# Second half's layernorm for the MLP made on x as features by tokens, with the tokens' moments sent through DRAM

## The chip, the cores and the metric

The kernel runs on one core of one Trainium2 chip. The metric is the device time of one execution in microseconds (us); the time shown for a kernel is the median of its runs. The core has five engines: TensorE (PE, with its weight loads shown apart as PEld), VectorE (DVE), ScalarE (ACT), GpSimd (POOL) and SyncE (SP). SP and POOL issue the DMA transfers here, each in the order of its own program.

## What is computed

The input x has 2048 tokens of 512 features, in fp32. Everything is made of its layernorm xn:

```python
xn = (x - mean(x)) / sqrt(var(x) + 1e-5)          # per token, over 512 features
a, b = xn @ Wd_re.T, xn @ Wd_im.T                 # DFT over the features
s = Ws_re @ a - Ws_im @ b                         # real part of the DFT over the tokens
g = silu((sigmoid(xn @ w_gate) * (xn @ w_up)) @ w_down)      # 512 -> 1792 -> 512
out = x + s * g
```

The MLP's matmuls contract over features, so xn is needed there with features on the partitions (features by tokens). The DFT over the tokens contracts over tokens, so there xn is needed with tokens on the partitions. The input array `x` is tokens by features; `x_t` holds the same x as features by tokens (8 pieces of 128 x 2 x 512) and before this change is read only for the residual at the end.

## The kernel before

**Arithmetic.** Every fp32 operand is split into a high part (`split`, L66, on ACT) and the rest (L67, on DVE), and a product is three matmuls of the parts (`mm3`, L70 to L72: high by high, high by rest, rest by high). Blocks of two by two are multiplied with seven products in place of eight; the sums and differences that this takes are DVE work (`combine`, L118; `x_sum`, L215).

**Stages.** Tokens come in two halves `h` of 1024, hidden features in seven groups `g` of 256. For half 0, group 0 is written out by hand (`start`), and its x is normalised and transposed there. Groups 1 to 6 of half 0 are six blocks (`block_units`) of nine units each, 54 units in all. Then come seven groups of half 1, the DFT over the tokens (`seq_units`) and the DFT over the features with the end (`hidden_units`).

**Order.** The program is a list of units written out by hand; a unit is 12 or 24 matmuls (a gate-up product `u1`, `u3`, `u5`, `u7`, `u8`, or a piece of the last group's down product, `carried`). `after(n, f)` puts the work `f` behind unit n, `sooner(n, f)` ahead of it. Ahead of each unit the loads of the next five units are issued and the operands of the next two are split. Engines run their own part of that program in order, and wait for each other through semaphores. All tiles in SBUF are 53 pages of 128 x 1024 fp32; a load waits until the page that it was given is free, so SP's queue runs ahead of the other engines as far as pages come free.

**The second half's x.** While half 0's blocks run, the eight tiles of 128 tokens of half 1 (`i` from 8 to 15) are prepared, two per block, around units m = 6, 15, 24 and 33 (the last lines of the kernel, L978 to L987):

- `fetch` (L147): loads x, tokens by features;
- `norm_a` (L155 to L158, behind unit m - 4): mean and variance on DVE into the tile `mv`, then on POOL the sum with eps (L157) and the power -0.5 (L158) into `rs`;
- `norm_b` (L163, behind unit m - 2): DVE makes (x - mean) * scale in place;
- `turn` (L176, behind unit m): four transposes on TensorE per tile, into a PSUM bank of the tag "pd". The down products use the same two "pd" banks;
- `keep_raw` (L187, behind unit m): ACT copies the bank into two pages `xraw[1, j, b]` (j is the pair of feature blocks, b the 512 tokens);
- `store_xn` (L169, behind unit m + 1): POOL stores the normalised tile to DRAM (`xn_part`) for the DFT over the tokens.

From unit 49 on, `xraw` is split and summed into half 1's operands (L66, L67, L215).

Of the kernel before, what the change touches and what calls it, by code (L numbers as in the profile page):

```python
# [8 lines left out]
F32 = mybir.dt.float32  # L9
F32R = mybir.dt.float32r  # L10
AF = mybir.ActivationFunctionType
ALU = mybir.AluOpType
ADD, SUB = ALU.add, ALU.subtract

P = 128
# [5 lines left out]
KH = NS // NH  # L21
NT = S // 512
SB = 512
# [8 lines left out]
def fnet_glu_kernel(ctx: ExitStack, tc: tile.TileContext, x, x_t, c_re, c_im, w_h, w_gu, w_down, out):  # L32
    nc = tc.nc
    PSUM = bass.MemoryType.PSUM

    const = ctx.enter_context(tc.tile_pool(name="const", bufs=1))
    stat = ctx.enter_context(tc.tile_pool(name="stat", bufs=4))
    pages = ctx.enter_context(tc.tile_pool(name="pages", bufs=PAGES))
    dram = ctx.enter_context(tc.tile_pool(name="dram", bufs=1, space=bass.MemoryType.DRAM))
    banks = ctx.enter_context(tc.tile_pool(name="banks", bufs=1, space=PSUM))  # L40

    def page(shape, dtype=F32R):
        return pages.tile([P, *shape], dtype, name="page")

    def bank(tag):
        return banks.tile([P, 512], F32, name=tag, bufs=2 if tag == "pd" else 1)
# [5 lines left out]
    mhalf = const.tile([P, 1], F32, name="mhalf")  # L52
    nc.gpsimd.memset(mhalf, -0.5)
    warm = const.tile([P, 1], F32, name="warm")
    nc.scalar.activation(warm, mhalf, AF.Sigmoid)
    xn_part = dram.tile([2, 2, 2, P, 4, D // 2], F32, name="xn_part")
    g_part = [dram.tile([P, 2, SB], F32, name=f"g_part{i}") for i in range(2 * NT)]
    ws_part = dram.tile([NG, 2, P, 2, 4 * P], F32, name="ws_part")
# [64 lines left out]
    xraw = {}  # L123
# [8 lines left out]
    def after(n, f):  # L132
        extra.setdefault(n, []).append(f)

    def sooner(n, f):
        early.setdefault(n, []).append(f)


    xs = {}

    def fetch(i, hold=False):
        pg = page([2, D], F32)
        if hold:
            nc.vector.memset(pg[:, 0, :1], 0.0)
        for j in range(2):
            xs[i + j] = pg[:, j, :]
            nc.sync.dma_start(xs[i + j], x[(i + j) * P : (i + j + 1) * P, :])  # L147

    st_of = {}

    def norm_a(i):
        st = stat.tile([P, 6], F32, name="st")
        mv = stat.tile([P, 2], F32, name="mv")
        rs = stat.tile([P, 2], F32, name="rs")
        nc.vector.bn_stats(st, xs[i])  # L155
        nc.vector.bn_aggr(mv, st)
        nc.gpsimd.tensor_scalar(rs[:, 0:1], mv[:, 1:2], EPS, None, op0=ALU.add)  # L157
        nc.gpsimd.tensor_tensor(rs[:, 1:2], rs[:, 0:1], mhalf, op=ALU.pow)  # L158
        st_of[i] = mv, rs

    def norm_b(i):
        mv, rs = st_of.pop(i)
        nc.vector.tensor_scalar(xs[i], xs[i], mv[:, 0:1], rs[:, 1:2], op0=ALU.subtract, op1=ALU.mult)  # L163

    def store_xn(i):

        q, p = divmod(i // 2, 4)
        to = xn_part[q, i % 2, :, :, p, :].rearrange("d p c -> p d c")
        nc.gpsimd.dma_start(to, xs.pop(i).rearrange("p (d c) -> p d c", d=2))  # L169
# [3 lines left out]
    def turn(i):  # L173
        turned[i] = bank("pd").rearrange("p (d s) -> p d s", d=ND)
        for d in range(ND):
            nc.tensor.transpose(turned[i][:, d, :], xs[i][:, d * P : (d + 1) * P], ident)  # L176

    def place(i):
        h, b, o = i // 8, i % 8 // 4, i % 4
        return [(h, j, b) for j in range(2)], slice(o * P, (o + 1) * P)  # L180

    def keep_raw(i):
        keys, at = place(i)
        for j, k in enumerate(keys):
            if k not in xraw:
                xraw[k] = page([2, SB], F32)
            nc.scalar.activation(xraw[k][:, :, at], turned[i][:, 2 * j : 2 * j + 2, :], AF.Copy)  # L187
# [17 lines left out]
    def x_sum(h, k):  # L205

        if (h, k) not in xsum:
            xsum[h, k] = page([2, SB], F32)
        a, b = {
            1: lambda: (xraw[h, 0, 1], xraw[h, 0, 0]),  # L210
            2: lambda: (xraw[h, 1, 1], xsum[h, 1]),
            3: lambda: (xraw[h, 1, 1], xraw[h, 0, 1]),
            4: lambda: (xraw[h, 1, 0], xsum[h, 2]),
        }[k]()
        nc.vector.tensor_tensor(xsum[h, k], a, b, op=SUB)  # L215
# [172 lines left out]
    class Seven:  # L388
# [56 lines left out]
        def run(self, k):  # L445
            first = k in (2, 1, 5)
            if first:
                self.ps = [bank("pd") for _ in range(2)]
            hv, wv = self.h[k].get(), self.weights(k)
            for o, ps in enumerate(self.ps):  # L450
                mm3(ps, [t[:, o * P : (o + 1) * P] for t in wv], hv, first, True, go_on=not first)
            (b, i), sign = {
                2: ((0, 0), 1),
                1: ((0, 0), 1),
                6: ((1, 0), -1),
                7: ((1, 1), -1),
                4: ((0, 1), 1),
                5: ((1, 1), 1),
                3: ((1, 0), 1),
            }[k]  # L460
            gather(0 if self.g == 0 and k in (2, 6, 7, 4) else 1, [((2 + b) * 2 + i, ps) for ps in self.ps], sign)
# [64 lines left out]
    def start(h, g):  # L526
# [43 lines left out]
        def begin():  # L570
# [7 lines left out]
            fetch(0)  # L578
            loads[0].load()
            norm_a(0)  # L580
            fetch(2, hold=True)
            loads[1].load()
            fetch(4)
            fetch(6)
            for p in units[0][0] + units[2][0]:
                p.load()
            wdl.load()
            norm_a(1)
            w_hi(0, 0)
            norm_b(0)  # L590
            turn(0)
            busy(2, 256)
            keep_hi(0)
            norm_b(1)
            turn(1)
            busy(4, 256)
            keep_hi(1)
            w_hi(0, 1)
            w_lo(0, 0)
            norm_a(2)  # L600
            w_lo(0, 1)
            norm_a(3)
# [49 lines left out]
    def c_blocks(tc_, pp):  # L652
        b = {(j, m): Load(c[tc_, j, pp], [2, SB]) for j in range(2) for m, c in enumerate((c_re, c_im))}
        return [b[k] for k in ((0, 0), (0, 1), (1, 0), (1, 1))]

    def xn_blocks(q):
        a = {(d, j): Load(xn_part[q, j, d], [4, D // 2]) for d in range(2) for j in range(2)}
        return [a[k] for k in ((0, 0), (0, 1), (1, 0), (1, 1))]
# [18 lines left out]
    def sums_ahead(n, make, blocks, to, at=(3, 5, 6, 8)):  # L677

        steps = make(*blocks, to)

        def step(dst, a, b, op, to):
            v = combine(dst(), a.get(), b.get(), op)
            nc.gpsimd.dma_start(to, v)

        for i, v in enumerate(blocks):
            sooner(n + i // 2, v.load)
        for i, v in enumerate(steps):
            after(n + at[i], lambda v=v: step(*v))
# [271 lines left out]
    with tc.manual_schedule():  # L960
        job, begin = start(0, 0)
        for i in range(KH):
            after(i // 2, lambda i=i: store_xn(i))
        for h in range(NH):
            n = len(units)
            for g in range(NG):
                m = len(units)
                if h and g:
                    job = late_units(h, g, job)
                elif h:  # L970
                    job = block_units(h, g, job, [], Seven(g))
                elif g:
                    job = block_units(h, g, job, [])
                if h == 0 and g in (1, 2):
                    sums_ahead(m, sums, c_blocks(0, g - 1), t_part[g - 1])
                elif h == 0 and g in (4, 5):
                    sums_ahead(m, diffs, xn_blocks(g - 4), s_part[g - 4])
            if h == 0:  # L978
                n = len(units)
                for i in range(KH):  # L980
                    m = 9 * (i // 2) + 6
                    if i % 2 == 0:
                        after(m - 6, lambda i=i: fetch(KH + i))
                    after(m - 4, lambda i=i: norm_a(KH + i))
                    after(m - 2, lambda i=i: norm_b(KH + i))
                    after(m, lambda i=i: (turn(KH + i), keep_raw(KH + i)))
                    after(m + 1, lambda i=i: store_xn(KH + i))  # L987
                for i, k in {-5: 1, -4: 2, 0: 6, 1: 5}.items():
                    sooner(n + i, xop[1, k].get)
                for i, k in {-3: 1, -2: 2, 1: 3, 2: 4}.items():  # L990
                    after(n + i, lambda k=k: x_sum(1, k))
            else:
                seq_units(job)
        hidden_units()
        begin()
        for n, (needs, run) in enumerate(units):
            now[0] = n
            for f in early.get(n, []):
                f()
            for k in range(n, min(n + LOAD_AHEAD + 1, len(units))):  # L1000
                for p in units[k][0]:
                    p.load()
            for k in range(n, min(n + SPLIT_AHEAD + 1, len(units))):
                for p in units[k][0]:
                    p.get()
            run()
            for f in extra.get(n, []):
                f()
# [52 lines left out]
```

## Time and profile before

| what | value |
|---|---|
| median of 3 runs | 821.48 us (821.05 to 822.24) |
| the profiled execution's own time | 822.36 us |
| its span, from the first to the last recorded instruction | 820.6 us |
| TensorE busy | 809.8 us, 99% of the span |
| VectorE / ScalarE / GpSimd busy | 645.2 / 490.9 / 144.0 us |
| DMA | 207.27 MB, mean 253 GB/s |
| granted TensorE clock | 0.999 |

"Busy" counts the instructions' own durations. Matmuls are pipelined: each is recorded for about 0.39 us but the next starts 0.227 us later, so the starts tell what a matmul costs, not the durations. Times in the views count from the start of the span; a "releaser" is what ended an engine's idle time; "landing" is the time from a DMA's issue to its arrival.

### The profile page before, as it was taken

Reading aid. Unit: us, or ns where it says so; the run is one execution under the profiler, and the core shown is the slowest. Engines: PE = TensorE matmul, PEld = TensorE weight load, DVE = VectorE, ACT = ScalarE, POOL = GpSimd, SP = SyncE. Lnnn points to the kernel's source line nnn. Section 1 sums busy time; section 2 is a strip of 40 time slices with the busy share of each in tenths; the row PEclk is TensorE's granted clock in tenths of the full one; section 3 lists DMA queues with packets and bytes.
Section 4 is the critical chain, followed back from the end, with each engine's and each line's share of the span. In section 5 each row is a group of like instructions: output and inputs, shape, how many; then the busy total and the mean of one; then the engine's idle time right before and its main releaser. Section 6 shows DMA issues by size and latency. Waiting matters only on the chain.

```text
span 820.6 us, 10472 instructions
## 1 busy us (share of the span) xinstructions
PE 809.8 (99%) x3686; PEld 673.2 (82%) x3686; DVE 645.2 (79%) x814; ACT 490.9 (60%) x762; POOL 144.0 (18%) x214
## 2 busy tenths in 40 slices
PE   8999999999999999999999999999999999999997
PEld 7988888888878888888888888888888888888786
DVE  6798867757788867876797796889888976988946
ACT  4666655655677888887787773544355545535441
POOL 2143422322111122212121100011101110002201
PEclk9999999999999999999999999999999999999999
DMA  8349999699677888998999997358937994799984
GB/s 317 144 170 401 272 257 285 186 321 309 163 175 165 228 179 214 251 200 199 280 291 311 265 347 271 134 209 309 310 146 287 341 394 150 253 316 395 304 275 77
DMA packets 59253, 207.27 MB, mean 253 GB/s; under 512 B 6592, under 2 KB 6848, under 8 KB 59200
## 3 DMA queue, kind: packets, MB, share of 16 engines
q0 software_dynamic: 25072, 87.57, 42.1%
q1 hardware_dynamic: 34128, 119.03, 40.2%
q8 instruction: 29, 0.48, 0.2%
q14 instruction: 24, 0.20, 0.1%
HBM read 122.16 MB, written 88.08 MB: 256 GB/s over the span
## 4 chain that ended last, share of the span: by engine, by line
PE 93%; DVE 3%; ACT 1%; DMA 1%; issue 1%; POOL 0%; SPq 0%; DVEq 0%
PE pd L70 6%; PE pd L71 6%; PE pd L72 6%; PE ga L70 5%; PE ga L72 5%; PE ua L72 5%; PE ua L71 5%; PE ga L71 5%; PE ua L70 5%; PE gc L70 3%; PE gc L72 3%; PE gc L71 3%; PE uc L72 3%; PE uc L70 3%; PE uc L71 3%; PE gb L72 3%
## 5 line engine op out<-in xcount | busy, mean ns | idle before, releaser
L67 DVE TENSOR_TENSOR page<-page 128x1024 fp32r<-128x1024 f32 (+1 forms) x340 | 322.0, 978 | 116.0 <-ACT page L66 114.5
L66 ACT ACTIVATE page<-page 128x1024 fp32r<-128x1024 f32 (+1 forms) x340 | 276.1, 859 | 91.8 <-DVE page L118 72.1
L118 DVE TENSOR_TENSOR page<-page 128x1024 f32<-128x1024 f32 (+2 forms) x184 | 169.2, 935 | 8.0 <-DMA page<-xn_part 5.9
L291 ACT ACTIVATE page<-pd 128x512 f32<-128x512 f32 x154 | 89.5, 595 | 62.7 <-PE pd L72 59.4
L295 POOL DMA_DIRECT2D g_part<-page x69 | 60.1, 889 | 277.2 <-ACT page L291 220.6
L70 PE MATMUL pd<-page 128*128 128x512 f32 x242 | 94.3, 390 | 0.8 <-DVE page L898 0.8
L71 PE MATMUL pd<-page 128*128 128x512 f32 x242 | 94.2, 389 | 0.0
L72 PE MATMUL pd<-page 128*128 128x512 f32 x242 | 94.2, 389 | 0.0
L70 PE MATMUL ga<-page 128*128 128x512 f32 x200 | 78.1, 391 | 0.8 <-ACT page L308 0.8
L72 PE MATMUL ga<-page 128*128 128x512 f32 x200 | 77.9, 390 | 0.0
L72 PE MATMUL ua<-page 128*128 128x512 f32 x200 | 77.9, 390 | 0.0
L71 PE MATMUL ga<-page 128*128 128x512 f32 x200 | 77.9, 389 | 0.0
L70 PE MATMUL ua<-page 128*128 128x512 f32 x200 | 77.9, 389 | 0.0
L71 PE MATMUL ua<-page 128*128 128x512 f32 x200 | 77.9, 389 | 0.0
L70 PEld LDWEIGHTS pd<-page 128*128 128x128 f32 x242 | 45.4, 188 | 10.7 <-issue 1.2
L72 PEld LDWEIGHTS pd<-page 128*128 128x128 f32 x242 | 45.4, 188 | 9.4
L71 PEld LDWEIGHTS pd<-page 128*128 128x128 f32 x242 | 45.4, 188 | 9.4
L70 PE MATMUL ub<-page 128*128 128x512 f32 (+1 forms) x126 | 48.3, 383 | 0.5 <-DVE page L940 0.5
L70 PE MATMUL gc<-page 128*128 128x512 f32 x124 | 48.6, 392 | 0.0
L71 PE MATMUL gc<-page 128*128 128x512 f32 x124 | 48.3, 390 | 0.0
L72 PE MATMUL gc<-page 128*128 128x512 f32 x124 | 48.3, 389 | 0.0
L70 PE MATMUL uc<-page 128*128 128x512 f32 x124 | 48.3, 389 | 0.0
(135 smaller groups left out, 1351.9 us busy)
## 6 DMA issues: line engine op xcount, KB each, us to landing
g_part<-page POOLq DMA_DIRECT2D x77, 512.0 KB, 7.8
page<-in_c_re_dram SPq DMA_DIRECT2D x36, 512.0 KB, 6.3
page<-f_part SPq DMA_DIRECT2D x36, 512.0 KB, 5.5
page<-in_c_im_dram SPq DMA_DIRECT2D x34, 512.0 KB, 6.0
page<-in_w_gu_dram SPq DMA_DIRECT2D x28, 512.0 KB, 7.6
f_part<-page POOLq DMA_DIRECT2D x28, 512.0 KB, 6.9
page<-in_w_down_dram SPq DMA_DIRECT2D x14, 512.0 KB, 8.7
page<-xn_part SPq DMA_DIRECT2D x14, 512.0 KB, 8.4
```

The source lines that it names most:

```text
L66: nc.scalar.activation(hi, src, AF.Copy)
L67: nc.vector.tensor_tensor(lo, src, hi.bitcast(F32), op=SUB)
L70: nc.tensor.matmul(ps, ws[0], ms[0], start=first, stop=False, skip_group_check=go_on)
L71: nc.tensor.matmul(ps, ws[0], ms[1], start=False, stop=False, skip_group_check=go_on)
L72: nc.tensor.matmul(ps, ws[1], ms[0], start=False, stop=last, skip_group_check=go_on)
L118: (engine or nc.vector).tensor_tensor(dst, a, b, op=op)
L291: nc.scalar.activation(pg[:, o, :], po, AF.Copy, scale=float(sign))
L295: nc.gpsimd.dma_start(g_part[i], pg, accum_op=ADD)
```

## The change

For half 1, `xraw` is no longer made by transposing the normalised tiles. It is loaded from `x_t` and normalised in place, features by tokens.

- `norm_a` for half 1 copies the mean on POOL (a new instruction) and writes the scale beside it, into a small tile `moments` of 128 x 2 x 8. `norm_b` and `store_xn` stay, with the mean and scale from `moments`.
- `turned_half(12, 0)` and `turned_half(30, 1)` prepare 512 tokens each. Behind unit 12 (30) POOL stores the means and the scales of four tiles to DRAM, `m_part[b]`: two DMAs of 128 x 4 single fp32 elements, each element to an address of its own, so that tokens lie in a row.
- Ten units later, ahead of unit 22 (40), SP issues three loads of 512 KB: `m_part[b]` to all 128 partitions (1024 values in each), and two pieces of `x_t`. They stand on SP's queue directly ahead of the w_gate and w_up loads for the next block.
- Behind units 26 to 29 (44 to 47) DVE does one 128 x 1024 operation each: minus the mean, times the scale, for both pieces.
- `turn` and `keep_raw` for half 1 go: 32 transposes on TensorE and 16 copies of 128 x 256 on ACT.

By the order of the built programs nothing else moves: DVE has 8 more instructions, POOL 8 copies and 4 DMAs more, SP 6 loads more.

```diff
+    moments = const.tile([P, 2, KH], F32, name="moments")
+    m_part = dram.tile([2, 2, SB], F32, name="m_part")
...
+        mean, scale = mv[:, 0:1], rs[:, 1:2]
+        if i >= KH:
+            mean, scale = (moments[:, m, i - KH : i - KH + 1] for m in range(2))
+            nc.gpsimd.tensor_scalar(mean, mv[:, 0:1], 0.0, None, op0=ALU.add)
         nc.gpsimd.tensor_scalar(rs[:, 0:1], mv[:, 1:2], EPS, None, op0=ALU.add)
-        nc.gpsimd.tensor_tensor(rs[:, 1:2], rs[:, 0:1], mhalf, op=ALU.pow)
-        st_of[i] = mv, rs
+        nc.gpsimd.tensor_tensor(scale, rs[:, 0:1], mhalf, op=ALU.pow)
+        st_of[i] = mean, scale
...
+    def turned_half(n, b):
+
+        both = Load(m_part[b].rearrange("m t -> (m t)").partition_broadcast(P).rearrange("p (m t) -> p m t", m=2), [2, SB])
+        raw = [Load(x_t[(2 + b) * 2 + j], [2, SB]) for j in range(2)]
+
+        def store():
+            at = slice(b * SB // P, (b + 1) * SB // P)
+            for m in range(2):
+                nc.gpsimd.dma_start(m_part[b, m].rearrange("(o p) -> p o", p=P), moments[:, m, at])
+
+        def step(j, m):
+            v = xraw[1, j, b] = raw[j].load()
+            by = both.load()[:, m, :].unsqueeze(1).to_broadcast([P, 2, SB])
+            nc.vector.tensor_tensor(v, v, by, op=(SUB, ALU.mult)[m])
+
+        after(n, store)
+        for v in (both, *raw):
+            sooner(n + 10, v.load)
+        for i in range(4):
+            after(n + 14 + i, lambda i=i: step(*divmod(i, 2)))
...
-                    after(m, lambda i=i: (turn(KH + i), keep_raw(KH + i)))
                     after(m + 1, lambda i=i: store_xn(KH + i))
+                turned_half(12, 0)
+                turned_half(30, 1)
```

More of the change, by code (lines that the diff above doesn't have):

```diff
@@ L156, in norm_a @@
         nc.vector.bn_aggr(mv, st)
+        mean, scale = mv[:, 0:1], rs[:, 1:2]
+        if i >= KH:
+            mean, scale = (moments[:, m, i - KH : i - KH + 1] for m in range(2))
+            nc.gpsimd.tensor_scalar(mean, mv[:, 0:1], 0.0, None, op0=ALU.add)
         nc.gpsimd.tensor_scalar(rs[:, 0:1], mv[:, 1:2], EPS, None, op0=ALU.add)
-        nc.gpsimd.tensor_tensor(rs[:, 1:2], rs[:, 0:1], mhalf, op=ALU.pow)
-        st_of[i] = mv, rs
+        nc.gpsimd.tensor_tensor(scale, rs[:, 0:1], mhalf, op=ALU.pow)
+        st_of[i] = mean, scale
     def norm_b(i):
-        mv, rs = st_of.pop(i)
-        nc.vector.tensor_scalar(xs[i], xs[i], mv[:, 0:1], rs[:, 1:2], op0=ALU.subtract, op1=ALU.mult)
+        mean, scale = st_of.pop(i)
+        nc.vector.tensor_scalar(xs[i], xs[i], mean, scale, op0=ALU.subtract, op1=ALU.mult)
+    def turned_half(n, b):
[14 more added lines that the diff above has]
+            after(n + 14 + i, lambda i=i: step(*divmod(i, 2)))
     def store_xn(i):
```

## The prediction

> **What bounds the kernel now.** I read the page first: span and busy time, the granted clock and DMA by slices, and the chain that ended last by engine.
>
> ```profile
> span 820.6 us, 10472 instructions
> PE 809.8 (99%) x3686; PEld 673.2 (82%) x3686; DVE 645.2 (79%) x814; ACT 490.9 (60%) x762; POOL 144.0 (18%) x214
> PEclk9999999999999999999999999999999999999999
> DMA  8349999699677888998999997358937994799984
> PE 93%; DVE 3%; ACT 1%; DMA 1%; issue 1%; POOL 0%; SPq 0%; DVEq 0%
> ```
>
> TensorE is the bound: 93% of the chain is its own work and it runs at full clock. The same could be an average over stages, so I read the view by stretches where most of the change lies.
>
> ```profile
> core 0: us, PE busy (x) PEld busy (x) DVE busy (x) ACT busy (x) POOL busy (x), PEclk, DMA share, GB/s
> 120.00:160.00 40.00, 40.00 (x186) 33.31 (x185) 28.97 (x47) 23.99 (x48) 13.37 (x19) 1.00 0.83 233
> 160.00:200.00 40.00, 40.00 (x178) 33.14 (x177) 29.65 (x44) 23.64 (x44) 9.00 (x14) 1.00 0.99 306
> ```
>
> TensorE has no gap from 120 to 200 us. DVE has some 10 of 40 us free, and DMA is full from 160 to 200 us (0.99). So an instruction taken from TensorE here is worth its spacing, unless what is added to DVE or DMA makes TensorE wait.
>
> **What goes: 32 transposes.** The view of the transposes' line from 40 to 160 us, then TensorE in order of time around the first eight:
>
> ```profile
> L176 PE MATMUL pd<-ident,page x32: 271/273/273, 61.8 to 155.0; 128*128 128x128 f32 x32
> ```
>
> ```profile
> 61.32 0.39 PE L71 MATMUL ua<-page 128*128 128x512 f32 x1
> 61.55 0.40 PE L72 MATMUL ua<-page 128*128 128x512 f32 x1
> 61.79 1.04 PE L176 MATMUL pd<-ident,page 128*128 128x128 f32 x8
> 62.58 0.48 PE L70 MATMUL gc<-page 128*128 128x512 f32 x1
> 62.89 0.39 PE L71 MATMUL gc<-page 128*128 128x512 f32 x1
> ```
>
> Matmuls start 0.227 us apart (61.32 to 61.55 and so on). From L71 at 61.32 to L71 at 62.89 is 1.57 us; without transposes it would be three spacings, 0.68 us. Eight transposes cost 1.57 - 0.68 = 0.89 us, 0.11 each, and not their recorded 0.273. The four places together: 4 x 0.89 = **3.55 us**. Nothing else hides there; the stretches show no gap of TensorE around them.
>
> Page and rule differ here. The Trainium skill, "TensorE: Matmul & The Clock Gate", section "Part 4: PE-mode transpose", gives about 275 ns for a transpose in a kernel; the recorded 273 ns agrees as a duration, and the spacing in this trace does not. By the page the sum would be 32 x 0.275 = 8.8 us.
>
> ACT loses 16 copies:
>
> ```profile
> L187 ACT ACTIVATE page<-pd x16: 373/390/408, 63.2 to 155.7; 128x256 f32<-128x256 f32 x16
> ```
>
> That is 16 x 0.39 = 6.2 us of an engine at 60%, off the path: counted as nothing, though it makes ACT earlier, never later.
>
> **What DVE gets: eight operations of 128 x 1024.** The nearest row is L118 in that shape:
>
> ```profile
> 102.49 1.22 DVE L118 TENSOR_TENSOR page<-page 128x1024 f32<-128x1024 f32 x1
> 103.63 1.29 DVE L67 TENSOR_TENSOR page<-page 128x512 fp32r<-128x512 f32 x2
> ```
>
> One takes 103.63 - 102.49 = 1.14 us of DVE's time, four 4.6 us. By the order of the built program the first four stand between 133.28 and 142.09 us, the second four between 195.82 and 201.42 us. Is there room?
>
> ```profile
> 139.26 0.69 DVE L274 TENSOR_TENSOR page<-page 128x512 fp32r<-128x512 f32 x1 [1.91 <-ACT page L273]
> ...
> 147.42 0.69 DVE L67 TENSOR_TENSOR page<-page 128x512 fp32r<-128x512 f32 x1 [3.52 <-ACT page L66]
> ```
>
> ```profile
> 195.82 1.29 DVE L67 TENSOR_TENSOR page<-page 128x512 fp32r<-128x512 f32 x2
> ...
> 208.59 1.83 DVE L67 TENSOR_TENSOR page<-page 128x1024 fp32r<-128x1024 f32 x2 [6.48 <-ACT page L66]
> ```
>
> Behind each group DVE idles (1.91 + 3.52 = 5.4 us, and 6.48 us), so it is back on time afterwards. What counts is what TensorE reads before that. The tightest is the first L67 at 195.82, behind one new operation: it ends at 196.50 and makes the rest part for the unit that starts here:
>
> ```profile
> 198.66 0.39 PE L70 MATMUL ga<-page 128*128 128x512 f32 x1
> 198.88 0.39 PE L71 MATMUL ga<-page 128*128 128x512 f32 x1
> ```
>
> Its first weight load of a rest part (for the third matmul) comes with the L71 at 198.88. The margin is 2.38 us, and 1.14 goes: cost 0, with 1.24 us left. If that cover is gone, each further microsecond of DVE delay costs one.
>
> **What POOL and SP get.** POOL, an engine at 18%: eight copies of 128 x 1, counted as nothing, and four stores of 512 single elements.
>
> ```profile
> 86.17 0.88 POOL L683 DMA_DIRECT2D t_part<-page  x1
> 90.97 0.87 POOL L295 DMA_DIRECT2D g_part<-page  x1 [3.92 <-ACT page L291]
> ...
> 147.80 0.89 POOL L683 DMA_DIRECT2D s_part<-page  x1
> ```
>
> ```profile
> L169 POOL DMA_DIRECT2D xn_part<-page x14: 720/732/869, 48.6 to 157.8; - x14
> ...
> DMA to landing us min/median/max: 3.3/6.3/11.3
> ```
>
> The nearest store is `xn_part` (two pieces per partition): 0.73 us to issue, 3.3 to 11.3 us to land. With four pieces per partition I estimate at most double, 1.5 us each; two fit into POOL's idle 3.92 us before 90.97. The first pair goes out at about 87 us and SP asks for it at 98.4 us (the issue of the next w_gate and w_up loads, below); the second at about 148.5 us, asked for at 164.5 us. At 11.3 us to landing SP would just not wait. I take 0. The Trainium skill, "DMA: Bandwidth & Descriptors", section "Rules for kernel authors", says that a last dimension that isn't contiguous gives one descriptor per element, and speaks against such stores; no row here shows one, and at 512 elements it bears on the rival below only.
>
> SP: three loads of 512 KB, twice. First place, ahead of the w_gate and w_up loads issued at 98.4 us (the view of those two, then DVE's first operation on them):
>
> ```profile
> L81 SPq DMA_DIRECT2D page<-in_w_gu_dram x2: 327/707/1087, 98.4 to 98.8; - x2
> ...
> DMA to landing us min/median/max: 6.6/7.8/9.1
> ```
>
> ```profile
> 122.97 0.69 DVE L118 TENSOR_TENSOR page<-page 128x512 f32<-128x512 f32 x1
> ```
>
> They land by 107.9 (98.8 + 9.1) and are first read at 122.97: a margin of 15 us, and no cost. Second place:
>
> ```profile
> 162.48 2.52 SPq L81 DMA_DIRECT2D page<-xn_part  x4
> 165.09 1.32 SPq L81 DMA_DIRECT2D page<-in_w_gu_dram  x2
> ```
>
> ```profile
> L81 SPq DMA_DIRECT2D page<-xn_part x4: 327/430/616, 162.5 to 164.5; - x4
> ...
> DMA to landing us min/median/max: 4.0/9.4/12.8
> ```
>
> ```profile
> L81 SPq DMA_DIRECT2D page<-in_w_gu_dram x2: 601/616/630, 165.1 to 165.8; - x2
> ...
> DMA to landing us min/median/max: 15.1/15.3/15.6
> ```
>
> ```profile
> 184.29 3.08 DVE L118 TENSOR_TENSOR page<-page 128x1024 f32<-128x1024 f32 x3
> 187.29 1.29 DVE L67 TENSOR_TENSOR page<-page 128x512 fp32r<-128x512 f32 x2
> ```
>
> ```profile
> 190.49 0.39 PE L70 MATMUL ga<-page 128*128 128x512 f32 x1
> ```
>
> The `xn_part` loads land from 166.5 (162.5 + 4.0) to 177.3 (164.5 + 12.8): three in 10.8 us, 3.6 us each. The two w_gate and w_up loads land by 181.4 (165.8 + 15.6): 4.1 us for two, 2.05 each. The new three stand between, and put the second w load off by 3 x 2.05 = 6.2 to 3 x 3.6 = 10.8 us. Operations of 128 x 512 start 0.60 us apart (one takes 0.69, two 1.29), so the third L118 above starts at 187.29 - 0.60 = 186.69; it is the first to read that load. I take 2.05, the rate at that very place: it lands at 187.6, and DVE waits 0.9 us. Cost on TensorE: the L67 at 187.29 feeds the unit at 190.49, whose first weight load of a rest part comes at 190.72, 2.75 us behind the end at 187.97, so nothing; at 195.82 the delays add up to 0.9 + 1.14 = 2.04 of 2.38 us, still nothing. At 3.6 us each DVE waits 192.2 - 186.69 = 5.5 us and TensorE loses 5.5 + 1.14 - 2.38 = 4.3 us.
>
> **Sum.** The profiled execution took 822.36 us (span 820.6 and 1.8 around it): 822.36 - 3.55 = 818.8. The median of the runs shown, 821.48, lies 0.88 below that execution, so the forecast for the median is 821.48 - 3.5 = **818.0 us**. The removed time is passed on to the end, since all later stages are TensorE's.
>
> **Rivals.** 0.2% is 1.64 us, about what a measurement of this kernel tells from no change: faster is below 819.84, slower above 823.12.
>
> 1. *The queue at 165 us is late* (a transfer takes the place of the transposes). At 2.8 us per load the w load lands at 189.9, DVE waits 3.2 us and TensorE loses 3.2 + 1.14 - 2.38 = 2.0 us: 820.0; with the bounds, 818.0 to 822.3 (full loss of 4.3). For it: DMA at 0.99 and `xn_part` at 3.6 us each. Against: the w loads' 2.05 directly behind.
> 2. *The moments hold up SP's queue: slower.* All 128 partitions read the same 4 KB of `m_part`, behind a store of single elements; no row shows either. The place is 165 us, since only there margins are short. If the stored moments and their load hold the queue for time H in place of 2.05 us, the second w load lands at 181.4 + H + 4.1 and TensorE loses 185.5 + H - 186.69 + 1.14 - 2.38 = H - 2.4. It turns at H = 6.0 (loss 3.55), and is slower by over 0.2% from H = 7.6. With H = 9, between that and the 12.8 us of the slowest load there: loss 6.6, 824.5; at 12.8, 828.3. For it: the unknown access. Against: 4 KB rows, as every other load, and stores with 11 to 16 us to land.
> 3. *The change doesn't do what it says*: the place of the transposes is filled by another wait (ACT's copies, or operands that come no sooner), so TensorE's work falls but its end doesn't: 821.5. Against it: not one gap in 120 to 200 us.
> 4. *A transpose is worth its recorded time*: 32 x 0.273 = 8.7 us, 812.7. The spacing above speaks against it; this is also the skill's figure.
>
> **How the numbers follow.** Forecast 0.57 (its own range 817.3 to 819.2); rival 1 0.18, half of it below 819.84; rival 2 0.15; rival 3 0.07; rival 4 0.03. Faster: 0.57 + 0.09 + 0.03 = 0.69, and 0.01 of rival 3: 0.70. Within: 0.09 + 0.06 = 0.15. Slower: 0.15. The range from 817.0 to 822.8 takes in the forecast and rivals 1 and 3 and leaves out rivals 2 and 4 (0.18).
>
> **What would show it.** Right: no L176 behind 40 us; TensorE still 40.00 of 40 us in each stretch; the chain's start of half 1 3.5 us earlier. New L67 or L118 waits on a DMA from `in_w_gu` around 183 to 190 us, with a gap of TensorE behind it, would show rival 1; a load of `m_part` with over 7 us to landing, or SP waiting for a store of `m_part`, rival 2; TensorE gaps without a DMA, rival 3. I am wrong if TensorE shows any new wait over 2 us between 50 and 240 us.

## Result and the profile after

The kernel after takes 825.38 us (median of 10 runs, 823.44 to 827.81), the kernel before 821.61 us in the same series (10 runs, 821.05 to 822.53). The ratio is 1.0046, 95% interval 1.0035 to 1.0057: slower by some 3.8 us, where 818.0 us were forecast. The profiled execution took 825.76 us.

The page of the kernel after, the lines that answer to those shown of before:

```profile
span 824.0 us, 10416 instructions
PE 808.5 (98%) x3654; PEld 670.9 (81%) x3654; DVE 653.8 (79%) x822; ACT 486.6 (59%) x746; POOL 149.4 (18%) x226
...
PE 88%; DVE 5%; DMA 3%; ACT 2%; issue 2%; POOL 0%; SPq 0%; DVEq 0%; ACTq 0%
```

The 32 transposes are gone (3686 - 32 = 3654 instructions on TensorE), and its busy time hardly falls. In the chain its share went from 93% to 88%; DVE and DMA took it over. (The lines of `after` named here stand two further down than in before: L72 to L74 are its `mm3`, L69 its rest parts, L120 its `combine`, L83 a load; in the kernels with a transpose of the moments everything is one line further.) The stretch from 160 to 200 us, whose columns are as in the prediction's view by stretches, shows how much:

```profile
160.00:200.00 40.00, 35.77 (x147) 29.04 (x146) 23.73 (x34) 19.55 (x36) 7.78 (x12) 0.91 1.04 355
```

Before, 178 matmuls start in these 40 us, now 147. The missing 31, at the 0.227 us of a matmul, are **7.0 us**. With the 3.55 us that the transposes gave this makes 7.0 - 3.55 = 3.5 us; the span grew by 824.0 - 820.6 = 3.4. So all of the result lies here, and this count is the measure for the runs below (run 11 alone loses more behind 200 us). The same shows when each matmul's start is set against that of the same matmul before: the kernel after is 0.3 us early at 60 us and 3.8 us from 160 to 180 us, so the four places gave 3.5 us; from 190 us to the end it is 3.2 us late. What made TensorE wait, from its view of waits (us in total, times, longest):

```profile
PE ga L74 <- DVE page L69: 4.2, 1, 4.2
```

and TensorE in order of time around that wait:

```profile
178.75 0.39 PE L73 MATMUL ga<-page 128*128 128x512 f32 x1
183.36 0.80 PE L74 MATMUL ga<-page 128*128 128x512 f32 x1 [4.23 <-DVE page L69]
...
187.37 0.63 PE L74 MATMUL ua<-page 128*128 128x512 f32 x1
187.79 0.63 PE L72 MATMUL gc<-page 128*128 128x512 f32 x1
...
188.91 0.39 PE L72 MATMUL gc<-page 128*128 128x512 f32 x1
189.14 0.39 PE L73 MATMUL gc<-page 128*128 128x512 f32 x1
```

From 178.75 to 183.36 nothing starts: 4.61 - 0.23 = 4.4 us. Then the matmuls start 0.42 us apart (187.37 to 187.79) until 188.65, and from there 0.23 again: TensorE runs at about half clock for 5 us. In the two stretches of 5 us behind 180 us the granted clock is 0.68 and 0.63:

```profile
180.00:185.00 5.00, 1.64 (x4) 1.35 (x5) 3.62 (x5) 1.06 (x3) 0.56 (x1) 0.68 1.04 360
185.00:190.00 5.00, 5.00 (x16) 3.90 (x15) 4.09 (x5) 3.33 (x7) 1.95 (x3) 0.63 1.05 398
```

The gap costs 4.4 us and the slow clock the rest of the 7.0, 2.6. The Trainium skill, "TensorE: Matmul & The Clock Gate", section "Part 1: The HAM clock gate (the "warmup" mystery)", says that the clock is halved after an idle window of about 3.4 us, and full again after about 3.4 us of work. Here the gap was 4.4 us, and matmuls ran at half clock for about 5 us. On the idle time the measurement differs: in run 4 below, a gap of 2.5 us, shorter than the page's window, has half clock behind it as well.

DVE was late with L69 since it waited itself:

```profile
180.88 1.83 DVE L120 TENSOR_TENSOR page<-page 128x1024 f32<-128x1024 f32 x2 [12.85 <-DMA page<-xn_part]
```

Before, this operation started after a wait of 5.95 us:

```profile
177.32 1.83 DVE L118 TENSOR_TENSOR page<-page 128x1024 f32<-128x1024 f32 x2 [5.95 <-DMA page<-xn_part]
```

`xn_part` is not what the change loads: these transfers stood in the program already. They are late because all transfers are, behind the second pair of the new stores of the moments. POOL's two stores to `xn_part` behind that pair land after 11.8 and 7.8 us (before 5.3 and 5.2), so SP issues the loads from 166.0 us on (before 162.5), and the last lands at 180.8 us. Before it landed at 177.3, which at this kernel's lead of 3.8 us would be 173.5: it is 7.3 us late. The view of `m_part`, which the change adds (POOL's stores, then SP's loads; the last line is for all six, and the four stores alone land after 13.8 to 14.1 us):

```profile
L179 POOL DMA_DIRECT2D m_part<-moments x4: 1064/1086/1107, 85.6 to 146.2; - x4
L83 SPq DMA_DIRECT2D page<-m_part x2: 330/342/355, 100.6 to 168.2; - x2
...
DMA to landing us min/median/max: 7.2/13.9/15.4
```

Here are the stretches of 5 us behind the two pairs of stores, first of before, then of after. The last two columns are the busy share of the DMA engines and GB/s:

```profile
95.00:100.00 5.00, 5.00 (x24) 4.14 (x23) 5.00 (x10) 3.47 (x7) 1.85 (x3) 1.00 1.00 366
150.00:155.00 5.00, 5.00 (x27) 4.20 (x26) 4.27 (x8) 3.06 (x7) 1.43 (x2) 1.00 0.79 193
155.00:160.00 5.00, 5.00 (x25) 4.17 (x24) 5.00 (x8) 3.47 (x9) 2.52 (x4) 1.00 1.02 311
```

```profile
95.00:100.00 5.00, 5.00 (x24) 4.14 (x23) 5.00 (x9) 3.18 (x6) 0.77 (x2) 1.00 0.97 46
150.00:155.00 5.00, 5.00 (x24) 4.14 (x23) 4.76 (x6) 1.81 (x4) 2.93 (x5) 1.00 1.27 71
155.00:160.00 5.00, 5.00 (x24) 4.14 (x23) 4.90 (x9) 3.24 (x7) 0.94 (x2) 1.00 0.68 50
```

Read the two columns together: from 95 to 100 us the engines are as busy as before (0.97 against 1.00), and move 46 GB/s in place of 366. 4 KB of moments hold up the transfers of half a megabyte each around them. POOL's own queue is not all that is held: two loads of x that SP issues at 86.0 and 86.4 us land after 13.0 and 13.3 us, and after 7.3 and 7.4 us in run 1 below, which issues them at the same time and has no stores of moments.

### The profile page after: what moved, and what is told of

Same layout as the page of the kernel before. It is cut to its first block, busy times and chain, and to the rows that moved or that the text cites. A ratio compares the mean times of both kernels' runs of the same rounds, so it can differ in the third digit from the quotient of the medians.

```text
span 824.0 us, 10416 instructions
## 1 busy us (share of the span) xinstructions
PE 808.5 (98%) x3654; PEld 670.9 (81%) x3654; DVE 653.8 (79%) x822; ACT 486.6 (59%) x746; POOL 149.4 (18%) x226
## 4 chain that ended last, share of the span: by engine, by line
PE 88%; DVE 5%; DMA 3%; ACT 2%; issue 2%; POOL 0%; SPq 0%; DVEq 0%; ACTq 0%
PE pd L72 6%; PE pd L74 6%; PE pd L73 6%; PE ga L74 5%; PE ga L72 5%; PE ua L72 5%; PE ua L73 5%; PE ua L74 5%; PE ga L73 5%; PE gc L72 3%; PE gc L73 3%; PE uc L72 3%; PE gb L72 3%; PE gc L74 3%; PE gb L73 3%; PE uc L73 3%
## 5 line engine op out<-in xcount | busy, mean ns | idle before, releaser
L69 DVE TENSOR_TENSOR page<-page 128x1024 fp32r<-128x1024 f32 (+1 forms) x340 | 321.7, 977 | 105.4 <-ACT page L68 104.0
L120 DVE TENSOR_TENSOR page<-page 128x1024 f32<-128x1024 f32 (+2 forms) x184 | 169.1, 934 | 14.9 <-DMA page<-xn_part 12.9
L72 PE MATMUL pd<-page 128*128 128x512 f32 x242 | 94.2, 389 | 0.8 <-DVE page L925 0.8
L74 PE MATMUL pd<-page 128*128 128x512 f32 x242 | 94.1, 389 | 0.0
L74 PE MATMUL ga<-page 128*128 128x512 f32 x200 | 78.5, 393 | 4.2 <-DVE page L69 4.2
L72 PE MATMUL ga<-page 128*128 128x512 f32 x200 | 78.3, 392 | 0.8 <-ACT page L335 0.8
L72 PE MATMUL ua<-page 128*128 128x512 f32 x200 | 78.3, 392 | 0.0
L74 PE MATMUL ua<-page 128*128 128x512 f32 x200 | 78.3, 391 | 0.0
L72 PEld LDWEIGHTS pd<-page 128*128 128x128 f32 x242 | 45.4, 188 | 10.5 <-issue 1.2
L74 PEld LDWEIGHTS pd<-page 128*128 128x128 f32 x242 | 45.4, 188 | 9.5
L72 PE MATMUL ub<-page 128*128 128x512 f32 (+1 forms) x126 | 48.3, 383 | 0.5 <-DVE page L967 0.5
L72 PE MATMUL gc<-page 128*128 128x512 f32 x124 | 48.5, 391 | 0.0
L74 PE MATMUL gc<-page 128*128 128x512 f32 x124 | 48.3, 389 | 0.0
L72 PE MATMUL uc<-page 128*128 128x512 f32 x124 | 48.3, 389 | 0.0
```

The lines of the kernel that those rows point to most:

```text
L69: nc.vector.tensor_tensor(lo, src, hi.bitcast(F32), op=SUB)
L72: nc.tensor.matmul(ps, ws[0], ms[0], start=first, stop=False, skip_group_check=go_on)
L74: nc.tensor.matmul(ps, ws[1], ms[0], start=False, stop=last, skip_group_check=go_on)
L120: (engine or nc.vector).tensor_tensor(dst, a, b, op=op)
```

## The experiments

Two theories stood at the start. **S** (the stores): stores of single elements hold the DMA engines, and `xn_part` comes late. **L** (the loads, the prediction's rival 1): three loads of 512 KB ahead of w_gate and w_up push these by up to 3.6 us each. Kernels that were run together on one chip share the runs of before, whose median is given; the count is that of matmuls from 160 to 200 us in the profiled execution.

**1. No stores.** The kernel after without the four stores; the broadcast reads 4 KB of x in their place, so the values that normalise `xraw` are not the moments.

```diff
-        both = Load(m_part[b].rearrange("m t -> (m t)")...
+        both = Load(x[2 * b : 2 * b + 2, :].rearrange("m t -> (m t)")...
...
-        after(n, store)
```

> The changed kernel without the four stores of single elements; the broadcast load takes its 4 KB per partition from the input x in place of m_part, so the values that half 1 is normalised with are not the moments. All loads, their places on SP's queue and the DVE operations stay. Theory S (the element stores hold the DMA engines, some 7 us per pair, and make xn_part late at 165 us): no DVE wait of 12.9 us on xn_part, no TensorE gap of 4.4 us, full clock, and 818.0 to 819.0 us. Theory L (the three more loads on SP's queue make it late): the gap stays, 824 to 827 us.

Measured: 823.19 us (822.58 to 825.43) against 821.77, ratio 1.0016 (1.0007 to 1.0025), 158 matmuls. The wait for `xn_part` is back to its old length, and a new one stands behind it:

```profile
174.02 1.83 DVE L120 TENSOR_TENSOR page<-page 128x1024 f32<-128x1024 f32 x2 [5.93 <-DMA page<-xn_part]
...
188.69 0.69 DVE L120 TENSOR_TENSOR page<-page 128x512 f32<-128x512 f32 x1 [5.28 <-DMA page<-in_w_gu_dram]
```

That is rival 1 at its upper bound: DVE waits 5.3 us for w_gate and w_up (5.5 were given for 3.6 us per load), and TensorE loses 20 x 0.227 = 4.5 us (4.3 were given). So S alone is not the cause: without the stores the gain is still lost.

**2. The stores alone.** The kernel before, with the moments copied and stored by elements, and nothing that loads them.

```diff
+        if i >= KH:
+            for m, v in enumerate((mv[:, 0:1], rs[:, 1:2])):
+                nc.gpsimd.tensor_scalar(moments[:, m, i - KH : i - KH + 1], v, 0.0, None, op0=ALU.add)
...
+                nc.gpsimd.dma_start(m_part[b, m].rearrange("(o p) -> p o", p=P), moments[:, m, at])
...
+                store_moments(12, 0)
+                store_moments(30, 1)
```

> The kernel before with the moments copied to a small tile and stored element by element at the same two places, and nothing else: transposes stay, nothing loads the moments. Theory S: the DMA rate falls below 100 GB/s for 7 to 8 us behind each pair of stores, the loads of xn_part land some 3 to 8 us later, DVE waits about 10 us in place of 5.9, TensorE gets a gap of 0 to 4 us; 822 to 828 us. Theory L: 821.6 us, within 0.2%.

Measured: 828.91 us (4 runs, 825.1 to 831.35) against 821.77, ratio 1.0079 (1.0055 to 1.0104): 7 us for 8 KB written that nobody reads. In the profiled execution, the longest of the four (831.35 us), TensorE starts 139 matmuls from 160 to 200 us, 39 fewer than before, or 8.9 us. Its wait is the one of the kernel after:

```profile
PE ga L74 <- DVE page L69: 5.8, 1, 5.8
```

**3. Pieces of 16 bytes.** The kernel after, with the four values of a partition stored side by side. The moments so come to other tokens than their own.

```diff
-                nc.gpsimd.dma_start(m_part[b, m].rearrange("(o p) -> p o", p=P), moments[:, m, at])
+                nc.gpsimd.dma_start(m_part[b, m].rearrange("(p o) -> p o", p=P), moments[:, m, at])
```

> The changed kernel with each partition's four elements stored as one piece of 16 bytes, so that the tokens' moments lie in another order in DRAM (half 1 is normalised with other tokens' moments). Same bytes, a quarter of the pieces. Theory S with a cost per piece: the DMA hold falls from 7 to 8 us to about 2 us per pair, no gap of TensorE over 1 us, 818 to 820 us. Theory S with a cost per store, whatever its pieces: 824 to 827. Theory L: 824 to 827.

Measured: 823.51 us (823.09 to 824.67) against 821.77, ratio 1.0021 (1.0012 to 1.003), 159 matmuls. The stores land after 7.7 us in place of 13.9, and the time is that of no stores at all. The long hold is gone; this does not tell yet whether because there are fewer pieces (128 in place of 512 per store), or because neighbouring words are now written in one piece.

**4. Moments turned on TensorE.** The whole computation: the 128 x 8 moments of a half are transposed once and stored as eight rows of 512 bytes.

```diff
-            for m in range(2):
-                nc.gpsimd.dma_start(m_part[b, m].rearrange("(o p) -> p o", p=P), moments[:, m, at])
+            pt = bank("pd")
+            nc.tensor.transpose(pt[:8, :P], moments[:, b].rearrange("p m o -> p (m o)"), ident)
+            nc.scalar.activation(rows[:, b], pt[:8, :P], AF.Copy)
+            nc.gpsimd.dma_start(m_part[b].rearrange("m (o p) -> (m o) p", p=P), rows[:, b])
...
-        after(n, store)
+        after(n + 3, store)
```

> The whole computation: the moments of four tiles (128 x 8) are transposed once on TensorE behind units 15 and 33, copied by ACT, and stored as 8 rows of 512 bytes. Theory S: the hold goes; two transposes cost about 0.5 us of the 3.55 us; 818.2 to 819.5 us. Theory L: 824 to 827 us.

Measured: 823.07 us (821.26 to 823.64) against 821.77, ratio 1.0011 (1.0002 to 1.002), 159 matmuls. The store lands after 5.2 us; DVE waits 4.1 us for w_gate, and TensorE 2.3 us, with half clock behind it. So three ways of taking the hold away end at the same 823 us: what is left should be L, which the next two runs test.

**5 and 6. The loads behind w_gate and w_up.** Kernel 4 with the three loads later (5), or with x early and only the broadcast late (6).

```diff
-            sooner(n + 10, v.load)
+            sooner(n + 12, v.load)
```

```diff
-        for v in (both, *raw):
-            sooner(n + 10, v.load)
+        for v in raw:
+            sooner(n + 5, v.load)
+        sooner(n + 12, both.load)
```

> The kernel with the moments turned on TensorE and stored as eight rows, and the three loads of each half issued two units later, so that SP issues them behind w_gate, w_up and w_down instead of ahead of them; nothing else differs. Theory L (the three loads push w_gate and w_up at 3.6 us each, and this is all that is left of the loss once the element stores are gone): w_gate lands near 178 instead of 185 us, the DVE wait on it (4.1 us) and the TensorE wait behind it (2.3 us, with the half clock after it) go, and the time falls from 823.1 to about 818.3 us (817.8 to 819.2), near the 3.5 us gain of the removed transposes. Rival B (the 1.5 MB are too much for the DMA engines in any order, or the eight DVE operations themselves cost the rest): the time stays within 822.3 to 823.8 us.

> The same kernel, with the two loads of x by features issued five units earlier than in the kernel after, ahead of the xn_part loads, into DMA engines that are little used at that time, and only the broadcast of the moments behind w_gate, w_up and w_down. Theory L: nothing of the change stands ahead of w_gate any more and only 512 KB stands behind it, so the time is that of the run with all three loads behind, 817.8 to 819.0 us. Rival (the early loads delay the xn_part loads or g_part stores, whose combine waits 5.9 us for them already before the change): the DVE wait on xn_part at 174 us grows by up to 7 us and the time stays at 821 us or more.

Measured: 819.01 us (818.53 to 819.94) and 819.23 us (818.43 to 819.65) against 821.99, ratios 0.9962 (0.9949 to 0.9976) and 0.9963 (0.9951 to 0.9976). Both are faster than both kernels, with the same transfers and DVE operations as kernel 4. The stretch of the first of them, and its w_gate and w_up loads:

```profile
160.00:200.00 40.00, 40.00 (x178) 33.14 (x177) 30.27 (x43) 22.39 (x42) 9.55 (x14) 1.00 1.01 325
```

```profile
L84 SPq DMA_DIRECT2D page<-in_w_gu_dram x2: 436/446/457, 163.1 to 163.6; - x2
...
DMA to landing us min/median/max: 14.2/15.2/16.1
```

178 matmuls, as before the change, at full clock. The loads now land by 163.6 + 16.1 = 179.7 us; in kernel 4 they took 21.0 and 21.4 us. Moving 1.5 MB on SP's queue by three places is worth 4 us: L holds. Rival B of the expectation falls: the same transfers and DVE operations, at the same DMA share of 1.01 as in kernel 4, no longer cost the time.

**7. Element stores, loads behind.** The kernel after with the edit of 5 and no other.

```diff
-            sooner(n + 10, v.load)
+            sooner(n + 12, v.load)
```

> The kernel after, element stores and all, with the three loads of each half issued two units later, behind w_gate, w_up and w_down. This leaves the element stores' hold alone. If hold and order each cost their own (theory S and L side by side): the DVE wait on xn_part stays near 12.9 us, TensorE still waits 3 to 4 us with a half clock behind it, and the time is 822 to 825 us, 0.5 to 3 us below the kernel after. If the order of the loads were the whole cause (theory L alone): 818.3 us. If the hold were the whole cause (theory S alone): no change from the kernel after, 825.4 us.

Measured: 825.13 us (823.83 to 826.34) against 821.99, ratio 1.0036 (1.0024 to 1.0049), 152 matmuls; DVE waits 12.5 us for `xn_part`, TensorE 3.9 us. By the interval this can't be told from the kernel after. So with the element stores left in, the order of the loads no longer decides: `xn_part` comes so late that w_gate, behind it, is no later than its readers (in the kernel after itself DVE has no wait for w_gate either). The two losses do not add up; either alone eats the gain. Of the four combinations, three lose it: loads ahead with stores by elements (825.4, the kernel after), loads ahead with stores by rows (823.1), loads behind with stores by elements (825.1). Only loads behind with stores by rows keeps it (819.0).

**8 to 10. What holds the engines: the small writes, or their neighbours?** Run 2 again, with the same 512 elements per store, each at a distance of 512, 64 and 16 bytes from the next in place of 4.

```diff
-    m_part = dram.tile([2, 2, SB], F32, name="m_part")
+    m_part = dram.tile([2, 2, SB, P], F32, name="m_part")      # 16 and 4 in place of P
...
-                nc.gpsimd.dma_start(m_part[b, m].rearrange("(o p) -> p o", p=P), moments[:, m, at])
+                nc.gpsimd.dma_start(m_part[b, m].rearrange("(o p) c -> p o c", p=P)[:, :, 0], moments[:, m, at])
```

> The kernel before, with the moments copied and stored by elements as in the earlier run of the stores alone, but each four-byte element goes to an address of its own 512 bytes from the next, where in that run the elements were neighbours. If each small write holds a DMA engine by itself: as in that run, 825 to 831 us, with the same hold of 7 to 8 us per pair of stores. If the cost comes from neighbouring elements written into the same piece of memory by different engines: near the kernel before, 821.8 to 823 us.

> The kernel before with the moments stored by elements and not loaded, each four-byte element 64 bytes from the next, where neighbours (4 bytes apart) gave 828.9 us and elements 512 bytes apart 822.3 us. If the hold comes from writes into the same 64 bytes: 821.8 to 823 us, with the stores landing 6 to 8 us after their issue. If it comes from writes into the same 512 bytes: above 823.5 us, with landings of 10 us and more.

> [...] If the hold grows with the writes that fall into the same 64 bytes: between the two, 822.5 to 827 us, with landings between 7 and 14 us. If only full neighbourhood counts: 821.8 to 823 us.

Measured, with the median landing of the four stores and the rate of all DMA from 95 to 100 us in the profiled execution:

| distance | time, us | before, us | ratio (95%) | stores land after, us | 95 to 100 us, GB/s |
|---|---|---|---|---|---|
| 4 bytes (run 2) | 828.91 | 821.77 | 1.0079 (1.0055 to 1.0104) | 14.3 | 61 |
| 16 bytes | 821.79 | 821.72 | 1.0003 (0.9993 to 1.0012) | 9.0 | 323 |
| 64 bytes | 821.93 | 821.72 | 1.0000 (0.9991 to 1.0009) | 6.6 | 365 |
| 512 bytes | 822.25 | 821.99 | 1.0003 (0.9994 to 1.0012) | 6.2 | 313 |

The view of the stores 4 bytes apart, and of those 64 bytes apart:

```profile
L174 POOL DMA_DIRECT2D m_part<-moments x4: 1072/1094/1115, 86.9 to 149.3; - x4
...
DMA to landing us min/median/max: 13.8/14.3/15.0
```

```profile
L174 POOL DMA_DIRECT2D m_part<-moments x4: 1067/1086/1107, 86.4 to 148.9; - x4
...
DMA to landing us min/median/max: 5.9/6.6/7.9
```

The issue costs POOL the same; the landing halves. So the number of small writes is not what costs the time: 512 elements far apart cost none. What counts is how near they lie: the time to landing falls from 14.3 to 9.0 and 6.6 us as 16, four and one of them fall into the same 64 bytes. The engines are not wholly free even then: from 154 to 156 us, behind the second pair, all DMA moves 14, 31 and 36 GB/s at 16, 64 and 512 bytes (135 before). But this passes within 2 to 4 us, where at 4 bytes the rate stays below 70 GB/s until 162 us. At 16 bytes the expectation of 822.5 us or more was missed: the landing lies between, as that theory had it, but the 2.4 us over 64 bytes are hidden. Why neighbours collide can't be seen in a trace. The distance also spreads the 512 elements of a store over more memory (2, 8, 32 and 256 KB), and no run changes the one without the other. The Trainium skill, "DMA: Bandwidth & Descriptors", section "Specifications", says that transfers under 512 bytes are done as read-modify-write. That neighbours wait for each other because of it is a possible reading, but no run shows it, and by itself it would hold at 64 bytes too, where these runs show no cost.

**11. A plainer repair.** Pieces of 16 bytes and loads behind (the edits of runs 3 and 7), with nothing on TensorE; DVE reads the moments back in the order of the tokens, in steps of 16 bytes.

```diff
-            by = both.load()[:, m, :].unsqueeze(1).to_broadcast([P, 2, SB])
-            nc.vector.tensor_tensor(v, v, by, op=(SUB, ALU.mult)[m])
+            by = both.load()[:, m, :].rearrange("q (p o) -> q o p", p=P).unsqueeze(1).to_broadcast([P, 2, SB // P, P])
+            w = v.rearrange("q k (o p) -> q k o p", p=P)
+            nc.vector.tensor_tensor(w, w, by, op=(SUB, ALU.mult)[m])
```

> The whole change with two edits and nothing on TensorE: each partition's four values of a moment stored side by side, as one piece of 16 bytes (the DVE operations read them back in the order of the tokens), and the three loads of each half behind w_gate, w_up and w_down. If the two causes found so far (neighbouring four-byte writes, loads ahead of w_gate) are all of the loss: 818.0 to 819.3 us, that is 3 us below the kernel before, as with the moments turned on TensorE and the loads behind. If pieces of 16 bytes still hold the DMA engines for 2 us or more, or the DVE operations get slower by reading in steps of 16 bytes (above 1.5 us each where 1.22 was measured): 820 us or more.

Measured: 820.95 us (819.29 to 823.17) against 821.72, ratio 0.999 (0.9981 to 0.9999): some 2 us above the expectation's first case, and within its second, that of slower DVE operations. The new line on DVE:

```profile
L185 DVE TENSOR_TENSOR page<-page x8: 1975/1994/2036, 129.9 to 206.4; 128x1024 f32<-128x1024 f32 x8
```

1.99 us each, where reading in a row takes 1.22; TensorE loses 9 matmuls from 160 to 200 us and 7 more from 200 to 240 us, 3.6 us in all in the profiled execution (822.47 us, 1.5 above the median). The Trainium skill, "SBUF — State Buffer", section "Door 1: The DMA port swizzle (why `[64,N]` ≈ `[32,N]`)", says that SBUF is read in lines of 16 bytes and that each step to a new line costs; this row agrees, though 16 bytes is the only step that was tried. To tell it from the stores, one more run:

**12. The same with plain reads.** Against run 11; tokens get each other's moments.

```diff
-            by = both.load()[:, m, :].rearrange("q (p o) -> q o p", p=P).unsqueeze(1).to_broadcast([P, 2, SB // P, P])
-            w = v.rearrange("q k (o p) -> q k o p", p=P)
-            nc.vector.tensor_tensor(w, w, by, op=(SUB, ALU.mult)[m])
+            by = both.load()[:, m, :].unsqueeze(1).to_broadcast([P, 2, SB])
+            nc.vector.tensor_tensor(v, v, by, op=(SUB, ALU.mult)[m])
```

> The kernel with pieces of 16 bytes and the loads behind, but the DVE operations read the moments as they lie, without steps (so tokens get each other's moments; all instructions and transfers stay). If the slower reads in steps of 16 bytes (2.00 us each where 1.22 was measured) cost what that kernel lacks of its expectation: 818.5 to 819.5 us. If the stores in pieces of 16 bytes cost it (they land after 7 us, a row of 512 bytes after 5.2): about 821 us, as with the steps.

Measured: 819.04 us (818.12 to 819.28) against 822.1, ratio 0.9964 (0.995 to 0.9977), 178 matmuls, DVE's operations back at 1.22 us. So the steps cost the 2 us, and stores in pieces of 16 bytes nothing. It also shows the gain, 3.1 us where 3.5 were forecast, in a kernel without any transpose of moments.

## Why the prediction was wrong

It forecast 818.0 us, and the time came out 7 us higher, outside the range and on the other side of before. The prediction's own sign of being wrong, a new wait of TensorE over 2 us, is the 4.2 us at 183 us.

- **What bounds the kernel** was read rightly: TensorE alone, with no gap from 120 to 200 us. A wait of TensorE there goes into the time in full, as 7.0 - 3.55 = 3.5 against 3.4 shows.
- **The transposes, 3.55 us**: the size was right. With both causes taken away the spans fall by 3.3 (run 5), 3.5 (run 6) and 4.3 us (run 12), and the times by 3.0, 2.8 and 3.1. Matmul by matmul, run 12 is 0.5 us early at 60 us and 4.0 at 160 us: 3.5 us. Rival 4's 8.7 us by recorded durations are out, and rival 3 too: TensorE's end does come sooner.
- **Eight DVE operations, no cost**: right. They take 1.22 us as recorded, as its nearest row did, and runs 5, 6 and 12 carry them without loss. That the margin was thin shows in run 11, where 0.77 us more each costs 2 us.
- **The element stores: "I take 0"**: this is the step that failed. The issue was within its bound (1.09 us against 1.5). The landing was not (13.9 against at most 11.3). But above all the step priced only the two ends of the store itself, POOL's issue and SP's wait for the result. It left out what every transfer has beside these: the time that it occupies the shared DMA engines while others queue. That this time was unknown had been said only for rival 2, at the place where SP reads the moments. The stores hit earlier, from about 150 us on, through `xn_part`, which the change doesn't touch and whose wait of 5.95 us in the trace of before left DVE no room; TensorE had some 2.9 us (7.3 us late, a gap of 4.4). The 0 was worth 7 us (run 2).
- **The loads at 165 us, 2.05 us each**: the mechanism was right, and the term was mis-sized by choosing the lower bound. In run 1 the second w_gate and w_up load lands 14.7 us after the last `xn_part` load (188.6 against 173.9), before the change 4.1 (181.4 against 177.3): put off by 10.6 us, 3.5 per load. The bounds were 6.2 to 10.8. The 2.05 came from loads directly behind the three slow ones, in a stretch where DMA was full; two landings close together at the end of a full queue are no rate for what is put in front of them. In the kernel after this loss doesn't show, since DVE has no wait for w_gate there; it shows once the stores no longer hold the engines.
- **TensorE's loss once it waits** was worked out as the delay less the margin, at full clock. The 5 us at half clock behind a gap of 4.4 us, 2.6 us of the loss, were not in the sum.
- **Rival 2** has the sign and nearly the time (824.5), but not the cause: its place was SP's queue waiting for the moments at 165 us. There they had landed before SP asked (the load is issued at 168.2 us, behind the late `xn_part` loads). SP did wait 13.5 us for them at the first place, around 100 us, where the margin of 15 us covered it. So the signs given for this rival did show (SP's wait, and loads of `m_part` that land after 7.2 and 15.4 us), though it is not the cause. A forecast by it would have been right by accident.

The range failed for the same reason as the forecast: it took its upper end from rival 1 alone, and the hold by the stores had no case of its own.

## What to carry to other kernels

A small strided store has three prices: issue, landing, and what it holds up for all others on the shared DMA engines; look at GB/s against the busy share right behind it. Keep words that different partitions write from lying side by side: turn them first, or give each partition a piece of 16 bytes, but then don't pay it back by reading in steps. A load that nobody needs soon belongs behind the ones that are waited for, and the price of standing ahead of them is the rate of the full queue, not the gap between its last two landings.

## What was not expected of the hardware

- A store of 512 four-byte elements, 4 bytes apart in DRAM, takes 14.3 us to land (run 2). Behind such pairs in the kernel after all DMA moves 46 GB/s from 95 to 100 us, and 71 and 50 from 150 to 160 us (366, 193 and 311 before). 64 bytes apart a store lands after 6.6 us and costs no time.
- After a gap of 4.4 us TensorE ran at half clock for 5 us (matmuls 0.42 us apart), and after one of 2.5 us for about 3.4 us (run 4); after one of 2.8 us in run 1 it did not (its clock from 160 to 200 us is 1.00). The length of the gap alone doesn't tell which.
- A DVE operation on 128 x 1024 with one operand read in steps of 16 bytes takes 1.99 us in place of 1.22.
